# ScalarE, VectorE and GpSimd in source order in blocks 2 to 10, with attention and the slot softmax cut into steps over sixteen columns

## The chip, the cores and the metric

The kernel runs on one core of a Trainium2 chip. TensorE (PE) multiplies, ScalarE (ACT) evaluates functions and copies, VectorE (DVE) does element work, reductions and 32x32 transposes, GpSimd (POOL) does element work and issues some loads, and the queue of SyncE (SP) issues most transfers. The metric is the device time of the program in microseconds (us). A profiled execution also has a span, from its first instruction to its last.

## The reference: what is computed

```python
# attention within chunks of 64 positions, for each of 8 x 8 heads; S = 576, D = 64
scores = (1 / sqrt(64)) * q_c @ k_c.T
attn   = softmax(scores, axis=-1)
x      = (attn @ v_c)                      # -> 4608 tokens x 512
# a feed-forward layer, d_ff = 2048
h = x @ w_in
x = (h * sigmoid(1.702 * h)) @ w_out
# soft mixture of experts, 8 experts x 4 slots
logits = x @ phi                           # 4608 x 32
d = softmax over the tokens (axis 0);  c = softmax over the slots (axis 1)
slot_out = per expert: relu((d.T @ x) @ w1) @ w2
out = c @ slot_out
```

## The kernel before

The 4608 tokens go in twelve blocks of 384. Blocks 0 and 1 are written out by hand (FIRST), together with the conversion of the weights; blocks 2 to 10 run in `block`, whose order is the subject here; block 11 and the expert part (`tail`) follow.

A block has sixteen **columns**, one for each 128 of the 2048 hidden features. In each, `gemm(b, f)` runs twelve matmuls into one of three PSUM banks h (the input is split into two parts, xh and xl, and the weight likewise, so three products for each of four slices of the depth). ScalarE evaluates a tanh of h into gt, VectorE multiplies gt with h (which frees h) and transposes the result into g1. After every fourth column g1 is written to DRAM, and a block later `load_g` reads it back in another layout.

After the gemm of a column, `side(b, f)` adds what the table PLAN names for it. Each entry is a letter, an index and the column:

- **a, b, c**: three steps of attention for one group of 128 tokens of the next block. `attn_a` makes the scores s on TensorE, the maximum mx and the difference e on VectorE, the exponential on ScalarE, the sum sm and reciprocal rs on VectorE, and the product with rs on GpSimd. `attn_b` transposes e on TensorE into pt, and ScalarE copies it to pt_sb. `attn_c` multiplies with v on TensorE into x; ScalarE writes xh from it, VectorE writes xl. Indices 0 to 4 count groups from the first of the next block, so a3 and a4 are already of the block after that.
- **l**: a quarter of the logits (lp); l3 is the last quarter of the block before. ScalarE and VectorE split its result into lps.
- **s0, s1**: the slot softmax of the block before: lg on TensorE, then nm, d, cr, dt, lt, cm on VectorE and ScalarE; s1 ends it and writes ct to DRAM.
- **g, d**: `load_g` of the block before, and `dispatch`, the product dtg of dt with what was read back; VectorE adds it to acc.
- **w**: alternately the load and the conversion of one piece of w_out (wo), on ScalarE and VectorE.

Two PSUM places are shared. The scores s and the product x use one pair of banks ("sx"), so s waits until xh and xl of the x before it are written, and x waits until e of the s before it is written. The tag "m" is one bank for lg, pt and dtg.

What orders the work: in blocks 2 to 10 SyncE and TensorE run in source order (`manual_schedule`), while a scheduler that works ahead of time decides the order on ScalarE, VectorE and GpSimd. In FIRST, in block 11 and in the tail only SyncE keeps source order. Each engine takes its instructions one after the other in the order so fixed.

Of the kernel before, what the change touches and what calls it, by code (L numbers as in the profile page):

```python
# [8 lines left out]
F32 = mybir.dt.float32  # L9
# [3 lines left out]
ACTF = mybir.ActivationFunctionType  # L13
ALU = mybir.AluOpType
AX = mybir.AxisListType

T = 384
# [7 lines left out]
TABLE = {'9.15': 'wxx', '10.6': 'q', '10.11': 'vq', '10.15': 'v', '11.0': 'ssw', '11.8': 'sss', 'a': 'ss', 'b': 'ssss', 'e': 'pppppp'}  # L25
TABLE.update({f'11.{f}': TABLE.get(f'11.{f}', '') + 'w' for f in range(1, 16)})
EVAC = 'vvvvvvvvvvvvvvaa'
LAST = (('g0', 2), ('l3', 4), ('l0', 4), ('s0', 5), ('d0', 7), ('s1', 7), ('l1', 12), ('l2', 12))


PLAN = (('g0', 3), ('a2', 4), ('l3', 4), ('l0', 4), ('b1', 4), ('c0', 4), ('s0', 5), ('w0', 6), ('s1', 7), ('w1', 7), ('a3', 8), ('d0', 8), ('c1', 8), ('b2', 8), ('a4', 12), ('l1', 12), ('l2', 12), ('b3', 12), ('c2', 12), ('w2', 14), ('w3', 15))
NCV = 6
FIRST = "q0 A0 q1 z Li0 A1 q2 Li1 q3 v0 Li2 i0 A2 B0 C0 v1 B1 C1 phi v2 i1 Li3 B2 C2 v3 A3 q4 Li4 i2 Li5 Li6 g0 Li7 g1 i3 Li8 i4 i5 q5 Li9 v4 i6 Li10 g2 g3 Li11 A4 i7 B3 g4 Li12 i8 C3 Lo0r q6 i9 g5 Li13 g6 i10 B4 q7 A5r Li14 i11 g7 o0 g8 i12 i13 g9 Lo1r C4 v5 Lo2r A6r Li15 i14 B5 Lo3 Lo4r i15 o1 g10 C5 g11 g12 g13 o2 Lo5r v6 Lo6 g14 Lo7r Lo8r s o3 g15 G0 o4 Lo9 Lo10r o5 Lo11r o6 G1 Lo12r A7 o7 Lo13r o8 G2 G3 v7 o9 B6 c0 o10 v8 Lo14 G4 o11 o12 C6 d0 G5 o13 c1 t0 Lo15 t1 o14 m0 G6 G7 G8 t2 t3 B7 d1 c2 q8 q9 G9 o15 t4 l0 d2 c3 G10 l1 C7 m1 l2 A8r G11 t5 d3 l3 t6 G12 v9 B8 t7 G13 S t8 G14 D1 t9 t10 t11 C8 t12 G15 T t13 t14 q10 m2 t15 D3 v10 A9 q11 B9 A10 q12"
EPS = 1e-9
# [3 lines left out]
def attention_moe_softmoe_kernel(  # L38
# [12 lines left out]
    nc = tc.nc  # L51
# [7 lines left out]
    NCP = T // 128  # L59
# [11 lines left out]
    st_p = ctx.enter_context(tc.tile_pool(name="st", bufs=2))  # L71
    ps_h = ctx.enter_context(tc.tile_pool(name="ps_h", bufs=3, space=bass.MemoryType.PSUM))
    ps = ctx.enter_context(tc.tile_pool(name="ps", bufs=1, space=bass.MemoryType.PSUM))
# [4 lines left out]
    def pair_tile(name):  # L78
        return ps_x[0].tile([128, 2, 512], F32, tag="sx", name=name)
# [7 lines left out]
    def mid_tile(shape, name, dtype=F32):  # L87
        return mid.tile(shape, dtype, tag="m", name=name)
# [7 lines left out]
    sel_r = sel.rearrange("p j s -> p (j s)")  # L96
# [60 lines left out]
    qk_t, v_t, et, pt, xh, xl = {}, {}, {}, {}, {}, {}  # L157

    def load_qk(cp):
        if cp < NB * NCP:  # L160
            t = qkp.tile([128, 2, KD, 128], F32, tag="qk", name="qk")
            nc.sync.dma_start(out=t, in_=qk[cp].rearrange("p (a h c) -> p a h c", a=2, h=KD))
            qk_t[cp] = t

    def load_v(cp):
        if cp < NB * NCP:
            t = vpool.tile([128, KD, 128], F32, tag="v", name="v")
            nc.sync.dma_start(out=t, in_=vs[cp].rearrange("p (h c) -> p h c", h=KD))
            v_t[cp] = t

    def attn_a(cp, pool=False):
        t = qk_t.pop(cp)
        p = pair_tile("s")[:, :, 0:256].rearrange("p h (a k) -> p h a k", k=64)
        for hp in range(KD):
            for c in range(2):
                w = slice(64 * c, 64 * c + 64)
                for h in range(2):
                    r = slice(64 * h, 64 * h + 64)
                    nc.tensor.matmul(  # L179
                        out=p[w, h, hp, :], lhsT=t[r, 0, hp, w], rhs=t[r, 1, hp, w], start=True, stop=True  # L180
                    )
        mx = st_p.tile([128, 2, KD, 1], F32, tag="mx", name="mx")
        e = mid_tile([128, 2 * KD, 64], "e")
        nc.vector.tensor_reduce(out=mx, in_=p, axis=AX.X, op=ALU.max)  # L184
        nc.vector.tensor_tensor(  # L185
            out=e.rearrange("p (a h) k -> p h a k", h=2), in0=p, in1=mx.to_broadcast([128, 2, KD, 64]),
            op=ALU.subtract,
        )
        nc.scalar.activation(out=e, in_=e, func=ACTF.Exp, scale=0.125)  # L189
        sm = st_p.tile([128, 2 * KD, 1], F32, tag="sm", name="sm")  # L190
        nc.vector.tensor_reduce(out=sm, in_=e, axis=AX.X, op=ALU.add)
        nc.vector.tensor_scalar_add(out=sm, in0=sm, scalar1=EPS)
        rs = st_p.tile([128, 2 * KD, 1], F32, tag="rs", name="rs")
        nc.vector.reciprocal(out=rs, in_=sm)  # L194
        (nc.gpsimd if pool else nc.vector).tensor_tensor(  # L195
            out=e, in0=e, in1=rs.to_broadcast([128, 2 * KD, 64]), op=ALU.mult
        )
        et[cp] = e

    def attn_b(cp):  # L200
        e = et.pop(cp)
        if cp in (1, 2):
            p = ps_h.tile([128, KD, 128], F32, tag="h", name="pt1")
        else:
            p = ps.tile([128, KD, 128], F32, tag="m" if cp >= 3 * NCP + 1 else "pt", name="pt")
        for hp in range(KD):
            nc.tensor.transpose(p[:, hp, :], e[:, 2 * hp:2 * hp + 2, :].rearrange("p h k -> p (h k)"), ident)  # L207
        t = ptp.tile([128, KD, 128], F32, tag="p", name="pt_sb")
        nc.scalar.activation(out=t, in_=p, func=ACTF.Copy)
        pt[cp] = t  # L210
# [57 lines left out]
    def load_g(b):  # L268
        g2[b] = []
        for q in range(NG):  # L270
            t = slab_tile([128, 4, NCP, GF * 32], F32, f"g2_{q}")
            nc.sync.dma_start(
                out=t.rearrange("p q a c -> p (q a c)"), in_=g_dram.pop((b, q)).rearrange("b p q x -> (b p) (q x)")
            )
            g2[b].append([t[:, :, i, :] for i in range(NCP)])
# [28 lines left out]
    lp, lps = {}, {}  # L304

    def logits(b, g):
        if g == 0:
            lp[b] = ps.tile([128, T], F32, tag="lp" if b % 2 else "pt", name="lp") if b else ps_h.tile([128, T], F32, tag="h", name="lp0")
        for j in range(4):
            f = 4 * g + j  # L310
            nc.tensor.matmul(  # L311
                out=lp[b][32 * j:32 * (j + 1), :], lhsT=wp[:, f, :], rhs=gt[b, f],
                start=(g == 0), stop=(g == NG - 1),
            )
        if g == NG - 1:
            p = lp.pop(b)
            if b == NB - 1:
                lps[b] = [mid_tile([128, T], "lps")]
                nc.scalar.activation(out=lps[b][0], in_=p, func=ACTF.Copy)
                return  # L320
            lps[b] = [mid_tile([128, T], f"lps{i}", F32R) for i in range(2)]
            nc.scalar.activation(out=lps[b][0], in_=p, func=ACTF.Copy)
            nc.vector.tensor_tensor(out=lps[b][1], in0=p, in1=lps[b][0].bitcast(F32), op=ALU.subtract)

    stat, lg_t, d_t, dt_t = {}, {}, {}, {}

    def slots_a(b):
        lg = ps.tile([128, T], F32, tag="m", name="lg")
# [78 lines left out]
    def dispatch(b):  # L407
        dt, cr = dt_t.pop(b)
        g = g2.pop(b)
        p = ps.tile([128, 512], F32, tag="m", name="dtg")  # L410
        for i in range(NCP):
            for j in reversed(range(4)):
                nc.tensor.matmul(  # L413
                    out=p[32 * j:32 * (j + 1)], lhsT=dt[:, i, :], rhs=g[j][i], start=(i == 0), stop=(i == NCP - 1)
                )
        nc.vector.scalar_tensor_tensor(out=acc, in0=acc, scalar=cr, in1=p, op0=ALU.mult, op1=ALU.add)  # L416
# [80 lines left out]
    def more_wo():  # L497
        fn, i = wo_list.pop(0)
        fn(i)
# [138 lines left out]
    def side(b, f):  # L638
        for name, at in (LAST if b == NB - 1 else PLAN):
            if f != at:  # L640
                continue
            kind, i = name[0], int(name[1:])
            if kind == "l":
                if i == NG - 1:
                    logits(b - 1, i)
                else:
                    logits(b, i)
            elif kind == "s":
                (slots_a, slots_b)[i](b - 1)
            elif kind == "d":  # L650
                dispatch(b - 1)
            elif kind == "g":
                load_g(b - 1)
            elif kind == "w":
                if 1 < b < 10:
                    more_wo()
            elif (b + 1) * NCP + i < NB * NCP:
                cp = (b + 1) * NCP + i
                if kind == "a":
                    attn_a(cp, True)  # L660
                    load_qk(cp + 2)
                elif kind == "b":
                    attn_b(cp)
                else:
                    attn_c(cp)
                    load_v(cp + 2)
# [35 lines left out]
    def block(b):  # L702
        for f in range(NF):
            gemm(b, f)
            side(b, f)
            if b == NB - 1 and f:
                gemm_t(b, f - 1)
            at(f"{b}.{f}")


    SP, PE = mybir.EngineType.SP, mybir.EngineType.PE
# [3 lines left out]
        with tc.tile_pool(name="pro", bufs=1) as pro[0]:  # L715
            start()
    with tc.tile_pool(name="spare", bufs=NSPARE) as pro[1]:
        with tc.manual_schedule(engines={SP, PE}):
            more_wo()
            for b in range(2, NB - 1):  # L720
                block(b)
        pair.__exit__(None, None, None)
        with tc.manual_schedule(engines={SP}):
            with tc.tile_pool(name="ps_t", bufs=1, space=bass.MemoryType.PSUM) as ps_x[0]:
                block(NB - 1)
                tail()
# [60 lines left out]
```

## Time and profile before

| what | value |
|---|---|
| time, median of 3 runs | 745.45 us (743.87 to 746.79) |
| the profiled execution's own time | 743.41 us |
| its span | 741.6 us |
| TensorE busy, share of the span | 656.0 us, 88% |
| VectorE busy | 445.5 us, 60% |
| ScalarE busy | 240.5 us, 32% |
| GpSimd busy | 107.5 us, 14% |
| mean granted TensorE clock | 0.965 |

Busy times overlap, since the engines work side by side. The end of the program is set by whichever engine the others wait for; a wait on that engine is time, a wait elsewhere is not. The granted clock is the share of TensorE's full rate that it was given.

### The profile page before, as it was taken

What the parts mean: (1) busy time and instruction counts of PE and PEld (TensorE: products, weight loads), DVE (VectorE), ACT (ScalarE), POOL (GpSimd) and SP (SyncE); (2) the same over time, 40 slices, a digit from 0 to 9 for tenths busy, and PEclk for the clock granted to TensorE, in tenths of its full rate; (3) what the DMA queues carried; (4) which work ended last, traced back from release to release, by engine and by line L of the source; (5) the groups of instructions that cost most, each with busy time, mean ns of one, the idle gap of its engine ahead of it and who ended that gap; (6) DMA issues with size and microseconds to landing.
All of it is one profiled execution on the core that took longest, in us unless ns stands there. A gap on an engine that the chain in (4) does not pass through costs nothing.

```text
span 741.6 us, 15661 instructions
## 1 busy us (share of the span) xinstructions
PE 656.0 (88%) x6462; PEld 536.4 (72%) x6462; DVE 445.5 (60%) x963; ACT 240.5 (32%) x517; POOL 107.5 (14%) x153
## 2 busy tenths in 40 slices
PE   3888999888998998989989989989899799988982
PEld 2777975666796896876968968968769689854641
DVE  6698762667557666676585576666765644531122
ACT  4466352523323332332333233323322222221132
POOL 1235000000100000000001000000000111435650
PEclk9998999999999999999999999999999999999997
DMA  7845264257657476575586574765855858979998
GB/s 246 324 179 207 86 241 157 58 145 267 189 131 261 140 215 230 132 277 146 132 279 178 126 257 147 225 219 130 280 142 163 281 155 294 342 269 324 385 393 367
DMA packets 64919, 161.66 MB, mean 218 GB/s; under 512 B 12880, under 2 KB 34512, under 8 KB 64848
## 3 DMA queue, kind: packets, MB, share of 16 engines
q1 hardware_dynamic: 54496, 123.43, 52.3%
q0 software_dynamic: 10352, 37.23, 13.8%
q8 instruction: 51, 0.84, 0.5%
q14 instruction: 20, 0.16, 0.1%
HBM read 119.14 MB, written 41.48 MB: 217 GB/s over the span
## 4 chain that ended last, share of the span: by engine, by line
PE 76%; DVE 8%; issue 6%; DMA 5%; ACT 2%; SPq 1%; POOL 0%; DVEq 0%; ACTq 0%; POOLq 0%
PE h L241 17%; PE h L242 16%; PE h L243 16%; PE dtg L413 6%; PE lp L311 5%; DMA g<-g_dram 3%; PE s L179 3%; PE pt L207 2%; PE x L225 2%; PE h1p L571 2%; DVE cv L107 1%; PE gtp L293 1%; DMA out_dram<-o 1%; DVE acc L416 1%; PE fp L591 1%
## 5 line engine op out<-in xcount | busy, mean ns | idle before, releaser
L241 PE MATMUL h<-xh,w 128*128 128x384 f32 x768 | 265.5, 346 | 2.7 <-DVE gt L246 2.0
L242 PE MATMUL h<-xl,w 128*128 128x384 f32 x768 | 260.4, 339 | 0.0
L243 PE MATMUL h<-xh,w 128*128 128x384 f32 x768 | 259.8, 338 | 0.0
L246 DVE SCALAR_TENSOR_TENSOR gt<-gt,h 128x384 f32<-128x384 f32 x192 | 105.6, 550 | 132.8 <-ACT gt L245 132.5
L245 ACT ACTIVATE gt<-h 128x384 f32<-128x384 f32 x192 | 94.0, 491 | 256.1 <-PE h L243 255.1
L241 PEld LDWEIGHTS h<-xh,w 128*128 128x128 f32 x768 | 146.1, 190 | 10.6 <-issue 4.4
L242 PEld LDWEIGHTS h<-xl,w 128*128 128x128 f32 x768 | 146.2, 190 | 1.2 <-issue 0.8
L243 PEld LDWEIGHTS h<-xh,w 128*128 128x128 f32 x768 | 146.0, 190 | 0.0
L195 POOL TENSOR_TENSOR e<-e,rs 128x512 f32<-128x512 f32 x28 | 30.1, 1075 | 454.2 <-DVE rs L194 454.2
L253 DVE STREAM_TRANSPOSE g<-gt 128x384 f32<-128x384 f32 x160 | 89.0, 569 | 3.6
L179 PE MATMUL s<-qk 64*64 64x64 f32 x1152 | 28.1, 242 | 34.3 <-issue 24.0
L179 PEld LDWEIGHTS s<-qk 64*64 64x64 f32 x1152 | 23.0, 150 | 44.5 <-issue 37.3
L413 PE MATMUL dtg<-g,dt 128*32 128x512 f32 x264 | 44.7, 831 | 5.2 <-DMA g<-g_dram 3.8
L189 ACT ACTIVATE e<-e 128x512 f32<-128x512 f32 x36 | 22.7, 631 | 66.1 <-DVE e L185 66.1
L225 PEld LDWEIGHTS x<-pt_sb,v 64*64 64x64 f32 x1152 | 21.9, 142 | 29.8 <-issue 20.0
L311 PE MATMUL lp<-gt,wp 128*32 128x384 f32 x384 | 40.7, 493 | 0.4 <-ACT wp L154 0.4
L225 PE MATMUL x<-pt_sb,v 64*64 64x64 f32 x1152 | 26.5, 232 | 13.1 <-PE pt L207 5.0
L475 POOL DMA_DIRECT2D w<-in_moe_w_dram x44 | 23.7, 543 | 91.2 <-PE x L225 26.0
L231 ACT ACTIVATE xh<-x 128x512 fp32r<-128x512 f32 x36 | 21.4, 595 | 39.0 <-PE x L225 39.0
L184 DVE TENSOR_REDUCE mx<-s 128x8 f32<-128x512 f32 x36 | 24.1, 670 | 16.3 <-PE s L179 16.3
L232 DVE TENSOR_TENSOR xl<-x,xh 128x512 fp32r<-128x512 f32 x36 | 24.4, 677 | 12.0 <-ACT xh L231 11.8
L413 PEld LDWEIGHTS dtg<-g,dt 128*32 128x32 f32 x264 | 10.1, 142 | 29.2 <-issue 27.0
(104 smaller groups left out, 603.0 us busy)
## 6 DMA issues: line engine op xcount, KB each, us to landing
g_dram<-g SPq DMA_DIRECT2D x160, 192.0 KB, 3.1
g<-g_dram SPq DMA_DIRECT2D x40, 768.0 KB, 8.4
qk<-in_qk_dram SPq DMA_DIRECT2D x36, 512.0 KB, 5.6
w<-in_moe_w_dram POOLq DMA_DIRECT2D x70, 256.0 KB, 5.2
w<-in_moe_w_dram POOLq DMA_DIRECT2D x27, 512.0 KB, 7.2
v<-in_v_dram SPq DMA_DIRECT2D x36, 256.0 KB, 5.8
stg<-in_moe_w_in_dram SPq DMA_DIRECT2D x16, 512.0 KB, 6.7
stg<-in_moe_w_out_t_dram SPq DMA_DIRECT2D x16, 512.0 KB, 5.6
```

The costliest lines, as they stand in the source:

```text
L179: nc.tensor.matmul(out=p[w, h, hp, :], lhsT=t[r, 0, hp, w], rhs=t[r, 1, hp, w], start=True, stop=True)
L195: (nc.gpsimd if pool else nc.vector).tensor_tensor(out=e, in0=e, in1=rs.to_broadcast([128, 2 * KD, 64]), op=ALU.mult)
L225: nc.tensor.matmul(out=x[64 * z:64 * z + 64, h, a, w], lhsT=t[r, 2 * a + z, w], rhs=p[r, 2 * a + z, w], start=True, stop=True,)
L232: nc.vector.tensor_tensor(out=yl, in0=x, in1=yh.bitcast(F32), op=ALU.subtract)
L241: nc.tensor.matmul(out=h, lhsT=a, rhs=xh[b][:, k, :], start=(k == 0), stop=False)
L242: nc.tensor.matmul(out=h, lhsT=a, rhs=xl[b][:, k, :], start=False, stop=False)
L243: nc.tensor.matmul(out=h, lhsT=l, rhs=xh[b][:, k, :], start=False, stop=(k == KD - 1))
L245: nc.scalar.activation(out=t, in_=h, func=ACTF.Tanh, scale=0.851)
L246: nc.vector.scalar_tensor_tensor(out=t, in0=t, scalar=1.0, in1=h, op0=ALU.add, op1=ALU.mult)
L253: nc.vector.transpose(out=g1[q][:, :, :, 32 * j:32 * (j + 1)], in_=t.rearrange("p (a b c) -> p b a c", b=4, c=32))
L311: nc.tensor.matmul(out=lp[b][32 * j:32 * (j + 1), :], lhsT=wp[:, f, :], rhs=gt[b, f], start=(g == 0), stop=(g == NG - 1),)
L413: nc.tensor.matmul(out=p[32 * j:32 * (j + 1)], lhsT=dt[:, i, :], rhs=g[j][i], start=(i == 0), stop=(i == NCP - 1))
```

## The change

All of ScalarE, VectorE and GpSimd now keep source order in blocks 2 to 10 as well. So that a step's later part does not stand in front of the next columns, the steps are cut: `attn_a` becomes `attn_s` (scores, maximum, difference; letter a) and `attn_e` (exponential to the product with rs; letter e), and the first half of the slot softmax becomes four functions `slots_0` to `slots_3` (letter S; S4 is the old `slots_b`). PLAN is written anew: its 21 entries stood in nine of the columns, 14 of them in columns 4, 8 and 12; its 27 entries now stand in thirteen. In LAST, the table of block 11, the dispatch moves from column 7 to column 9.

```diff
-LAST = (('g0', 2), ('l3', 4), ('l0', 4), ('s0', 5), ('d0', 7), ('s1', 7), ('l1', 12), ('l2', 12))
-PLAN = (('g0', 3), ('a2', 4), ('l3', 4), ('l0', 4), ('b1', 4), ('c0', 4), ('s0', 5), ('w0', 6), ('s1', 7), ('w1', 7), ('a3', 8), ('d0', 8), ('c1', 8), ('b2', 8), ('a4', 12), ('l1', 12), ('l2', 12), ('b3', 12), ('c2', 12), ('w2', 14), ('w3', 15))
+LAST = (('g0', 2), ('l3', 4), ('l0', 4), ('s0', 5), ('s1', 7), ('d0', 9), ('l1', 12), ('l2', 12))
+PLAN = (('b1', 1), ('w2', 1), ('w3', 1), ('g0', 2), ('a2', 2), ('l3', 3), ('l0', 3), ('e2', 3), ('c0', 4), ('S0', 5), ('a3', 6), ('S1', 6), ('b2', 7), ('e3', 7), ('S2', 7), ('c1', 8), ('S3', 8), ('S4', 9), ('a4', 10), ('d0', 10), ('b3', 11), ('e4', 11), ('c2', 12), ('l1', 12), ('l2', 12), ('w0', 13), ('w1', 13))
...
     def attn_a(cp, pool=False):
+        attn_s(cp)
+        attn_e(cp, pool)
+
+    def attn_s(cp):
...
+        et[cp] = e
+
+    def attn_e(cp, pool):
+        e = et[cp]
...
+    def slots_0(b):
+        lg = ps.tile([128, T], F32, tag="m", name="lg")
+        for i, v in enumerate(lps.pop(b)):
+            nc.tensor.matmul(out=lg, lhsT=sel_r, rhs=v, start=(i == 0), stop=(i == 1))
+        nm = st_p.tile([128, 1], F32, tag="nm", name="nm")
+        nc.vector.tensor_reduce(out=nm, in_=lg, axis=AX.X, op=ALU.max, negate=True)
+        nc.vector.tensor_tensor(out=nm, in0=nm, in1=stat[b - 1][0], op=ALU.min)
+        lt = st_p.tile([128, NCP, 32], F32, tag="lt", name="lt")
+        for j in range(4):
+            r = slice(32 * j, 32 * j + 32)
+            nc.vector.transpose(out=lt[r], in_=lg[r, :].rearrange("p (a j c) -> p a j c", j=4, c=32)[:, :, j, :])
+        sm_t[b] = lg, nm
+        lg_t[b] = lt
+
+    def slots_1(b):
+        lg, nm = sm_t.pop(b)
+        s = st_p.tile([128, 1], F32, tag="sum", name="sum")
+        d = mid_tile([128, T], "d")
+        nc.scalar.activation(out=d, in_=lg, func=ACTF.Exp, bias=nm, accum_out=s)
+        cr = st_p.tile([128, 1], F32, tag="cr", name="cr")
+        nc.scalar.activation(out=cr, in_=stat[b - 1][0], func=ACTF.Exp, scale=-1.0, bias=nm)
+        sm_t[b] = d, nm, s, cr
+
+    def slots_2(b):
+        d, nm, s, cr = sm_t.pop(b)
+        dt = st_p.tile([128, NCP, 32], F32, tag="dt", name="dt")
+        for j in range(4):
+            r = slice(32 * j, 32 * j + 32)
+            nc.vector.transpose(out=dt[r], in_=d[r, :].rearrange("p (a j c) -> p a j c", j=4, c=32)[:, :, j, :])
+        nc.vector.scalar_tensor_tensor(out=s, in0=stat[b - 1][1], scalar=cr, in1=s, op0=ALU.mult, op1=ALU.add)
+        dt_t[b] = dt, cr
+        stat[b] = nm, s
+        lt = lg_t[b]
+        cm = st_p.tile([128, NCP, 1], F32, tag="cm", name="cm")
+        nc.vector.tensor_reduce(out=cm, in_=lt, axis=AX.X, op=ALU.max)
+        nc.vector.tensor_tensor(out=lt, in0=lt, in1=cm.to_broadcast([128, NCP, 32]), op=ALU.subtract)
+
+    def slots_3(b):
+        nc.scalar.activation(out=lg_t[b], in_=lg_t[b], func=ACTF.Exp)
...
+            elif kind == "S":
+                (slots_0, slots_1, slots_2, slots_3, slots_b)[i](b - 1)
...
                 if kind == "a":
-                    attn_a(cp, True)
+                    attn_s(cp)
                     load_qk(cp + 2)
+                elif kind == "e":
+                    attn_e(cp, True)
...
-        with tc.manual_schedule(engines={SP, PE}):
+        with tc.manual_schedule(engines={SP, PE, mybir.EngineType.Activation, mybir.EngineType.DVE, mybir.EngineType.Pool}):
```

What the instructions' order becomes is shown at three places. Line numbers are those of each kernel's own file, so tanh is L245 before and L253 now.

**ScalarE, from the columns before column 4 to column 8 of a middle block.** `gt<-h` is the tanh of one column (x8: eight columns), `xh<-x` belongs to c0 of column 4. Before:

```order
L245 ACTIVATE gt<-h 128x384 x8
L322 ACTIVATE lps_3594<-lp 128x384
L189 ACTIVATE e<-e 128x512
L209 ACTIVATE pt_sb<-pt 128x512
L245 ACTIVATE gt<-h 128x384
L103 ACTIVATE wo<-wo_3458 128x512
L351 ACTIVATE d,sum<-lg,nm 128x384
L355 ACTIVATE cr<-nm 128x1
L245 ACTIVATE gt<-h 128x384 x2
L377 ACTIVATE lt<-lt 128x96
L245 ACTIVATE gt<-h 128x384
L231 ACTIVATE xh<-x 128x2x2x128
```

and now:

```order
L253 ACTIVATE gt<-h 128x384 x2
L330 ACTIVATE lps_3582<-lp 128x384
L198 ACTIVATE e<-e 128x512
L253 ACTIVATE gt<-h 128x384
L239 ACTIVATE xh<-x 128x2x2x128
L253 ACTIVATE gt<-h 128x384 x2
L354 ACTIVATE d,sum<-lg,nm 128x384
L356 ACTIVATE cr<-nm 128x1
L253 ACTIVATE gt<-h 128x384
L217 ACTIVATE pt_sb<-pt 128x512
L198 ACTIVATE e<-e 128x512
L253 ACTIVATE gt<-h 128x384
```

The copy of c0 to xh stood behind the tanh of column 8, four tanhs after that of column 4; it now stands right behind the tanh of column 4, and the slot softmax's `d` one tanh later than the column of its lg.

**VectorE, columns 5 to 8 of a middle block.** `gt<-gt,h` is the multiplication that frees a bank h, `g<-gt` the transposition, `xl<-x,xh` the second half of an attention step c. Before (from the slot softmax on):

```order
L246 SCALAR_TENSOR_TENSOR gt<-gt,h 128x384
L376 TENSOR_TENSOR lt<-lt,cm 128x96
L246 SCALAR_TENSOR_TENSOR gt<-gt,h 128x384
L383 TENSOR_REDUCE cs<-lt 128x3
L384 TENSOR_SCALAR cs<-cs 128x3
L385 RECIPROCAL cs<-cs 128x3
L386 TENSOR_TENSOR lt<-lt,cs 128x96
L388 STREAM_TRANSPOSE ct_b<-lt 128x96
L246 SCALAR_TENSOR_TENSOR gt<-gt,h 128x384
L253 STREAM_TRANSPOSE g_3558<-gt 128x12x32 x2
L232 TENSOR_TENSOR xl<-x,xh 128x2x2x128
L253 STREAM_TRANSPOSE g_3558<-gt 128x12x32 x2
L253 STREAM_TRANSPOSE g_3748<-gt 128x12x32
```

and now (column 7 to the step c of column 8):

```order
L254 SCALAR_TENSOR_TENSOR gt<-gt,h 128x384
L261 STREAM_TRANSPOSE g_3614<-gt 128x12x32
L200 TENSOR_REDUCE sm<-e 128x8
L201 TENSOR_SCALAR sm<-sm 128x8
L203 RECIPROCAL rs<-sm 128x8
L364 STREAM_TRANSPOSE dt<-d 32x96 x4
L365 SCALAR_TENSOR_TENSOR sum<-sum,cr 128x1
L370 TENSOR_REDUCE cm<-lt 128x3
L371 TENSOR_TENSOR lt<-lt,cm 128x96
L254 SCALAR_TENSOR_TENSOR gt<-gt,h 128x384
L261 STREAM_TRANSPOSE g_3773<-gt 128x12x32
L240 TENSOR_TENSOR xl<-x,xh 128x2x2x128
```

Before, the xl of column 4 came behind the slot softmax and two transpositions of later columns. Now column 7 holds the multiplication, the transposition, the sum of an attention step (sm, rs) and the dt half of the slot softmax, and the xl shown last is that of c1 in column 8.

**VectorE, the start of block 2.** The rows begin with the maximum of A10, the last attention step of FIRST, and end with the product of e with rs that b1 needs. Before:

```order
L184 TENSOR_REDUCE mx<-s 128x8
L185 TENSOR_TENSOR e<-s,mx 128x2x4x64
L246 SCALAR_TENSOR_TENSOR gt<-gt,h 128x384 x2
L253 STREAM_TRANSPOSE g_1788<-gt 128x12x32
L191 TENSOR_REDUCE sm<-e 128x8
L253 STREAM_TRANSPOSE g_1788<-gt 128x12x32
L192 TENSOR_SCALAR sm<-sm 128x8
L246 SCALAR_TENSOR_TENSOR gt<-gt,h 128x384
L194 RECIPROCAL rs<-sm 128x8
L253 STREAM_TRANSPOSE g_1788<-gt 128x12x32
L195 TENSOR_TENSOR e<-e,rs 128x512
```

and now:

```order
L189 TENSOR_REDUCE mx<-s 128x8
L190 TENSOR_TENSOR e<-s,mx 128x2x4x64
L254 SCALAR_TENSOR_TENSOR gt<-gt,h 128x384
L261 STREAM_TRANSPOSE g_1788<-gt 128x12x32
L200 TENSOR_REDUCE sm<-e 128x8
L254 SCALAR_TENSOR_TENSOR gt<-gt,h 128x384
L201 TENSOR_SCALAR sm<-sm 128x8
L261 STREAM_TRANSPOSE g_1788<-gt 128x12x32
L203 RECIPROCAL rs<-sm 128x8
L204 TENSOR_TENSOR e<-e,rs 128x512
L105 TENSOR_SCALAR wo<-wo 128x512
L108 SCALAR_TENSOR_TENSOR wo<-wo_1770,wo 128x512
```

Between A10's difference and its product there stood three multiplications and three transpositions of block 2; now there are two of each. The conversion of wo (the last two rows) stood ahead of the step before, A9, and now stands behind A10. TensorE's order changes with it: b1, which needs A10's product, stood behind five gemms of block 2 (column 4) and now stands behind two (column 1), directly after A10's scores; and A9's transposition, which had ten matmuls of the third gemm of block 2 ahead of it, now stands behind the second gemm.

## Rows read from the trace of the kernel before

**Rows 1.** Waits of TensorE over the whole span: us in total, times, longest.

```profile
PE s L179 <- issue: 24.0, 8, 3.0
PE x L225 <- PE pt L207: 5.0, 8, 0.6
PE dtg L413 <- DMA g<-g_dram: 3.8, 1, 3.8
```

**Rows 2.** Chain of work, middle block: start us, us, what.

```profile
331.56 3.01 issue
334.56 0.69 PE s L179 x32
335.26 4.45 PE dtg L413 x24
339.73 0.76 DVE acc L416
350.21 1.43 PE lp L311 x16
352.24 0.61 issue
353.54 0.37 PE h L241
353.91 0.18 PE h L242
```

**Rows 3.** The same chain, ten microseconds earlier.

```profile
322.00 0.67 PE x L225 x32
```

**Rows 4.** Timeline of ScalarE in that block.

```profile
331.58 0.49 ACT L245 ACTIVATE gt<-h 128x384 f32<-128x384 f32 x1 [0.40 <-PE h L243]
331.96 0.59 ACT L231 ACTIVATE xh<-x 128x512 fp32r<-128x512 f32 x1
```

**Rows 5.** Timeline of VectorE in that block.

```profile
333.81 0.65 DVE L232 TENSOR_TENSOR xl<-x,xh 128x512 fp32r<-128x512 f32 x1
343.96 0.56 DVE L246 SCALAR_TENSOR_TENSOR gt<-gt,h 128x384 f32<-128x384 f32 x1 [2.29 <-ACT gt L245]
344.55 0.58 DVE L253 STREAM_TRANSPOSE g<-gt 128x384 f32<-128x384 f32 x1
352.05 0.69 DVE L185 TENSOR_TENSOR e<-s,mx 128x512 f32<-128x512 f32 x1
353.72 0.68 DVE L191 TENSOR_REDUCE sm<-e 128x8 f32<-128x512 f32 x1
378.43 1.11 DVE L362 STREAM_TRANSPOSE dt<-d 32x96 f32<-32x96 f32 x4
```

**Rows 6.** Stretches: us, busy PE, PEld, DVE, ACT, POOL; clock; DMA share; GB/s.

```profile
333.00:334.00 1.00, 0.00 (x0) 0.00 (x0) 1.00 (x3) 0.00 (x0) 0.00 (x0) 1.00 0.43 164
336.00:337.00 1.00, 1.00 (x12) 0.32 (x8) 0.97 (x2) 0.00 (x0) 0.00 (x0) 0.50 0.72 164
162.00:164.00 2.00, 1.63 (x9) 1.63 (x10) 2.00 (x5) 0.52 (x1) 0.00 (x0) 1.00 0.49 197
```

**Rows 7.** Chain of work in block 11: the last dispatch.

```profile
664.02 2.90 PE dtg L413 x24
```

**Rows 8.** Timeline of TensorE at the start of block 2.

```profile
158.73 0.66 PE L207 MATMUL pt<-ident,e 128*128 128x128 f32 x4 [0.33 <-DVE e L195]
159.67 0.69 PE L179 MATMUL s<-qk 64*64 64x64 f32 x32
162.37 0.44 PE L241 MATMUL h<-xh,w 128*128 128x384 f32 x1 [2.00 <-DVE gt L246]
```

**Rows 9.** Timeline of VectorE there: A10's product.

```profile
165.37 0.65 DVE L195 TENSOR_TENSOR e<-e,rs 128x512 f32<-128x512 f32 x1
```

**Rows 10.** Line L424, the load of wo: from issue to landing.

```profile
DMA to landing us min/median/max: 4.0/4.7/5.8
```

**Rows 11.** Line L272, the strips read back by load_g: from issue to landing.

```profile
DMA to landing us min/median/max: 5.3/8.4/13.0
```

More of the change, by code (lines that the diff above doesn't have):

```diff
@@ L197, in attn_a @@
         )
-        et[cp] = e
     def attn_b(cp):
@@ L323, in logits @@
             nc.vector.tensor_tensor(out=lps[b][1], in0=p, in1=lps[b][0].bitcast(F32), op=ALU.subtract)
-    stat, lg_t, d_t, dt_t = {}, {}, {}, {}
+    stat, lg_t, d_t, dt_t, sm_t = {}, {}, {}, {}, {}
+    def slots_0(b):
[34 more added lines that the diff above has]
+        nc.scalar.activation(out=lg_t[b], in_=lg_t[b], func=ACTF.Exp)
     def slots_a(b):
```

## The prediction

> **What bounds the kernel now.** I read first who TensorE waits for over the whole span, then the chain of work of one middle block, then the timelines of the engines that the chain names, and last the granted clock in short stretches.
>
> The waits of TensorE [rows 1] are few kinds: the scores s of the attention waited 24.0 us in eight waits of some 3 us, the product x 5.0 us in eight, and one dispatch 3.8 us for a transfer. In blocks 2 to 9 one wait of each of the first two kinds stands in each block. In the chain [rows 2] the first is the "issue" of 3.01 us, just before the scores of a3 in column 8. The chain names no releaser, the other views do: the scores need the banks in which x of c0 lies. That x was computed at 322.00 [rows 3], but ScalarE copied it to xh only at 331.96 [rows 4], behind the tanh of column 8 at 331.58, and VectorE's xl ended at 333.81 + 0.65 = 334.46 [rows 5], 0.10 us before the scores start. So TensorE waits for the place of two instructions in two queues, not for their work. The wait of 0.61 us before an x [rows 2] ends 0.10 us after VectorE's e of the scores just before it, at 352.05 + 0.69 = 352.74 [rows 5]: the same pair of banks, the other way round.
>
> The long wait costs more than itself. [...] An idle time of 2.00 us at the start of block 2 [rows 8] left the clock at 1.00 [rows 6].
>
> **What comes back.** The copies to xh and xl now stand directly behind their own x, no longer behind four later tanhs.
>
> - a3 stands two columns behind c0. Two gemms of twelve matmuls at 0.17 to 0.18 us [rows 2] are 4.2 us; xh and xl need about 1.4 (0.59 and 0.65 with the hand-overs). The eight waits go: 24.0 us.
> - Without that idle time I take the dispatch at full clock: 4.45 - 2.90 = 1.55 us, in nine blocks 14.0 us. In block 10 the idle time is the wait for the transfer, so it must go as well.
> - That transfer (the strips of load_g) is issued one column earlier and needed two columns later. Eight gemms, 16.8 us, lie between, and the slowest strip took 13.0 us [rows 11]: 3.8 us come back.
> - No x stands directly behind the scores any more; at least one gemm lies between: 5.0 us.
> - The dispatch is no longer followed by a transposition that needs its bank back; the 0.76 us of VectorE's acc [rows 2] leave the chain, and an x of 0.67 us [rows 3] that ran beside it enters: 0.1 us, in nine blocks 0.9.
>
> Together 47.7 us.
>
> **What it costs.**
>
> - *More changes of shape.* The first gemm matmul after an x takes 0.37 us, the next 0.18 [rows 2]. Before, two groups of side work in a block ended with x. Now two x (columns 4 and 8) and two groups of logits (3 and 12) are followed by a gemm, and two scores (2 and 6), whose 64x64 matmuls are nearest to x. Four more at 0.2 us, in nine blocks: 7.2 us. The bounds are two more (only logits and x cost it: 3.6) and seven more (transpositions, lg and dispatch too: 12.6).
> - *The start of block 2.* A10's scores ended at 159.67 + 0.69 = 160.36 [rows 8] and its product at 165.37 + 0.65 = 166.02 [rows 9], 5.66 us later. One multiplication and one transposition less lie in between (0.56 + 0.58 [rows 5]), so 4.5 us; and b1, which needs the product, now stands directly behind the scores. TensorE idles 4.5 us there instead of 2.00. A9's transposition waited 0.33 us [rows 8]; the ten matmuls that stood ahead of it (1.7 us) are gone, and A9's product comes earlier by the conversion of wo (about 1.1 us, an estimate from two element rows such as 0.56 and 0.65): it waits 0.6 longer. That is 3.1 us. The idle time is longer than 3.01, so I add one fall of the clock, 1.55, and the sum is 4.7. At best, if the product came sooner, it is 0.
> - *The quarter l0 in column 3* now stands directly behind the gemm whose gt it needs. Tanh and multiplication take 0.49 + 0.56 [rows 4, 5], with hand-overs 1.15; TensorE meanwhile does l3 and three quarters of l0, seven eighths of 1.43 [rows 2], so 1.25. Nothing, but the cover is only 0.1 us.
> - *VectorE in column 7.* Multiplication, transposition, sm and dt are 0.56 + 0.58 + 0.68 + 1.11 [rows 5], and six short ones I put at 0.9 (an estimate): 3.8 us against 2.7 of TensorE. The xl of c1 comes 0.56 + 0.58 + 0.65 later and is needed by a4. Counted from the end of gemm 7, VectorE starts at 0.6 and is done at 6.2; TensorE comes to a4 after a transposition, three gemms and an x, 0.66 + 6.3 + 0.67 = 7.6. The cover is 1.4 us, from which some 0.4 of backlog of column 5 goes.
> - GpSimd's products have at least three columns until the transposition that needs them: nothing.
>
> [...] The new table makes more and smaller groups. [...]
>
> **The sum.** 47.7 - 7.2 - 4.7 = 35.8 us. The profiled execution took 743.41 us, its span 741.6 and 1.8 around it; it becomes 707.6. It lies 2.0 below the median of the runs, 745.45, which becomes **709.7 us**.
>
> **The rivals.**
>
> - *VectorE is late after column 7.* Some thirty instructions of it stand between column 5 and the xl of c1; if each took 0.08 us longer than I lay them, 2.4 us, the cover of about 1.0 is used up and a4 waits 1.4 us in eight blocks: 11 us, 721 us. For it: the column's sum is above TensorE's. Against it: columns 8 to 10 leave room. [...]
> [...]
> - *It does little*: the scores wait for something other than xl, and the waits stay where they are: some 745 us. Against it stand the two hand-overs of 0.10 us.
> - *Slower: the load of wo holds up ScalarE in column 1.* That load is issued behind the conversion of column 13, about 2.8 us after gemm 13 ends, and ScalarE comes to the conversion in column 1 after four gemms, a transposition and a copy, at 9.6: the load has 6.8 us. It took 4.0 to 5.8 [rows 10]. In source order a late load holds back the tanh behind it, then gt, then l0, almost one for one. If it took as long as the slowest strip, 13.0 [rows 11], that is 6.2 us in the seven blocks 3 to 9, 43 us: 753 us. It turns the sign from 12.1 us on, where 7 x 5.3 exceeds 35.8.
> - *Better*: only logits and x cost the 0.2 (3.6 back) and the start of block 2 hides half: 703 us and below.
>
> **Chances.** Forecast (703 to 716) 0.60; VectorE late 0.17; clock 0.07; better 0.08; little 0.04; slower 0.04. The range 700 to 723 holds the forecast, most of VectorE's case and the better one, some 8 in 10. A change within 0.5% (3.7 us) is about what a measurement of this kernel cannot tell from none. Faster 0.92, same 0.04, slower 0.04.
>
> **What the changed profile would show.** The 3 us waits before the scores are gone; xh starts within a microsecond of its x; the dispatch takes 2.9 us and the clock stays at 1.00 through the middle blocks; a middle block is some 4.5 us shorter (40.5 in nine). One wait of 4 to 5 us stands at the start of block 2, before b1. No dispatch waits for a strip. The forecast would be wrong if TensorE waited in each block for VectorE before a4 or before l0, or for a gt behind a late conversion of wo, or if the first matmul after each small group cost clearly more than 0.2 us.

## The result, and the profile after the change

The changed kernel takes 705.33 us (median of 4 runs, 704.88 to 708.01); the kernel before, run beside it, 745.19 us (median of 4, 743.87 to 746.79). The ratio is 0.9472, interval 0.9441 to 0.9502: 39.9 us less. The profiled execution went from 743.41 to 708.01 us (35.4 less), its span from 741.6 to 706.2. The forecast was 709.7 by the median and 707.6 for the profiled execution.

The page of the changed kernel: TensorE is now busy for 92% of the span (88% before), with nearly the same busy time, and the row of its granted clock has a 9 in all slices but two, the one in which block 2 starts (8) and the last (7). The mean granted clock is 0.982 (0.965 before).

```profile
PE 652.3 (92%) x6462; PEld 534.7 (76%) x6462; DVE 446.6 (63%) x963; ACT 238.7 (34%) x517; POOL 107.3 (15%) x153
...
PEclk9999999998999999999999999999999999999997
```

TensorE's waits over the whole span (us in total, times, longest). None of the three lines of [rows 1] is left. The longest line now, 8.4 us for two loads of qk, was there before with 7.8. The new one holds the 5.1 us at the start of block 2:

```profile
PE pt L215 <- DVE e L204: 6.0, 2, 5.1
```

One stretch of 47 us in the middle blocks: TensorE is busy all of it, at a clock of 1.00 (columns as in [rows 6]). A wait between the matmuls of one group, as that of l0 further down, does not show as idle time here.

```profile
294.00:341.00 47.00, 47.00 (x458) 40.25 (x459) 33.92 (x75) 15.64 (x32) 3.13 (x3) 1.00 0.67 211
```

The chain of a middle block, from the scores of column 2 to those of the next block (start us, us, what; most of the twelve gemm matmuls of a column are left out). It is TensorE from end to end.

```profile
307.07 0.62 PE s L184 x32
307.69 0.38 PE h L249
...
309.98 2.00 PE lp L319 x16
311.98 0.37 PE h L249
...
314.26 0.62 PE x L233 x32
314.89 0.38 PE h L249
...
317.18 0.35 PE lg L339 x2
317.52 0.17 PE h L249
...
319.61 0.62 PE s L184 x32
320.23 0.38 PE h L249
...
322.52 0.44 PE pt L215 x4
322.95 0.18 PE h L249
...
325.06 0.63 PE x L233 x32
325.69 0.38 PE h L249
...
330.06 0.62 PE s L184 x32
330.68 2.71 PE dtg L462 x24
333.40 0.37 PE h L249
...
338.85 1.43 PE lp L319 x16
340.28 0.37 PE h L249
...
353.43 0.62 PE s L184 x32
```

Three things are to be seen. The scores of a3 and a4 (319.61, 330.06) follow their gemm without a wait, where [rows 2] have 3.01 us. The dispatch takes 2.71 us against 4.45. And 353.43 - 307.07 = 46.36 us is one block; before, the 3.01 us "issue" stood at 331.56 [rows 2] and again at 382.58, 51.02 us later. More rows of the chain before, with that block's transpositions:

```profile
340.63 0.63 PE pt L207 x4
...
351.63 0.60 PE pt L207 x4
...
372.43 0.59 PE pt L207 x4
...
382.58 3.01 issue
```

ScalarE's timeline beside it: xh follows its x at 314.26 by 0.08 us after x ends (314.88); [rows 3, 4] had almost ten microseconds between the two.

```profile
314.96 0.60 ACT L239 ACTIVATE xh<-x 128x512 fp32r<-128x512 f32 x1 [0.16 <-PE x L233]
```

### The profile page after: what moved, and what is told of

It is laid out like the page before. It is cut to its first block, busy times and chain, and to the rows that moved or that the text cites. A ratio compares the mean times of both kernels' runs of the same rounds, so it can differ in the third digit from the quotient of the medians.

```text
span 706.2 us, 15678 instructions
## 1 busy us (share of the span) xinstructions
PE 652.3 (92%) x6462; PEld 534.7 (76%) x6462; DVE 446.6 (63%) x963; ACT 238.7 (34%) x517; POOL 107.3 (15%) x153
## 4 chain that ended last, share of the span: by engine, by line
PE 79%; DVE 7%; DMA 7%; issue 2%; ACT 2%; POOL 1%; DVEq 0%; POOLq 0%; ACTq 0%
PE h L249 20%; PE h L250 18%; PE h L251 18%; PE lp L319 6%; PE dtg L462 4%; DMA w<-in_moe_w_dram 4%; PE s L184 3%; PE x L233 3%; PE pt L215 2%; PE gtp L301 1%; DMA qk<-in_qk_dram 1%; DVE cv L108 1%; DMA out_dram<-o 1%; POOL w L530 1%; PE dtg L449 1%
## 5 line engine op out<-in xcount | busy, mean ns | idle before, releaser
L249 PE MATMUL h<-xh,w 128*128 128x384 f32 x768 | 271.7, 354 | 0.7 <-ACT xh L239 0.7
L251 PE MATMUL h<-xh,w 128*128 128x384 f32 x768 | 260.4, 339 | 0.0
L253 ACT ACTIVATE gt<-h 128x384 f32<-128x384 f32 x192 | 94.1, 491 | 311.1 <-PE h L251 311.0
L261 DVE STREAM_TRANSPOSE g<-gt 128x384 f32<-128x384 f32 x160 | 92.5, 578 | 5.2
L319 PE MATMUL lp<-gt,wp 128*32 128x384 f32 x384 | 45.9, 493 | 0.4 <-ACT wp L155 0.4
L524 POOL DMA_DIRECT2D w<-in_moe_w_dram x44 | 23.6, 541 | 61.5 <-PE h L251 28.4
L462 PE MATMUL dtg<-g,dt 128*32 128x512 f32 x264 | 30.6, 596 | 1.4 <-DVE dt L407 1.4
L215 PE MATMUL pt<-ident,e 128*128 128x128 f32 x144 | 23.9, 292 | 8.5 <-DVE e L204 6.0
L530 POOL DMA_DIRECT2D w<-in_moe_w_dram x53 | 28.3, 537 | 17.9 <-DMA w<-in_moe_w_dram 11.8
```

The lines of the kernel that those rows point to most:

```text
L249: nc.tensor.matmul(out=h, lhsT=a, rhs=xh[b][:, k, :], start=(k == 0), stop=False)
L251: nc.tensor.matmul(out=h, lhsT=l, rhs=xh[b][:, k, :], start=False, stop=(k == KD - 1))
L253: nc.scalar.activation(out=t, in_=h, func=ACTF.Tanh, scale=0.851)
L261: nc.vector.transpose(out=g1[q][:, :, :, 32 * j:32 * (j + 1)], in_=t.rearrange("p (a b c) -> p b a c", b=4, c=32))
L319: nc.tensor.matmul(out=lp[b][32 * j:32 * (j + 1), :], lhsT=wp[:, f, :], rhs=gt[b, f], start=(g == 0), stop=(g == NG - 1),)
L462: nc.tensor.matmul(out=p[32 * j:32 * (j + 1)], lhsT=dt[:, i, :], rhs=g[j][i], start=(i == 0), stop=(i == NCP - 1))
```

## The experiments

In the first four the question is which part of the change does it and whether VectorE's cover is as thin as the forecast says; in the others, what its two visible costs are.

**The old table in source order.** The kernel before, with only the list of engines changed.

```diff
-        with tc.manual_schedule(engines={SP, PE}):
+        with tc.manual_schedule(engines={SP, PE, mybir.EngineType.Activation, mybir.EngineType.DVE, mybir.EngineType.Pool}):
```

> The table and the whole steps of the kernel before, with ScalarE, VectorE and GpSimd in source order in blocks 2 to 10. Theory (order and table are both needed): the copies xh and xl of c0 stand behind their x, so the 3 us wait before a3 goes; but the whole attention step and the whole slot softmax now stand in front of the next columns on VectorE, and in columns 4, 8 and 12 a product x stands right behind the scores of the same column, so x waits for VectorE's e there, several us in column 8. I expect 730 to 755 us, no clear gain. Rival (the order alone is the gain, the table is ornament): about 710 us.

771.00 us (769.51 to 772.18), ratio 1.0362 (1.0333 to 1.0391): slower than expected. A block takes 54.5 us. TensorE's waits, then ScalarE's timeline around column 7, and VectorE's and TensorE's in column 8:

```profile
PE x L225 <- issue: 26.8, 9, 3.8
PE pt L207 <- DVE acc L416: 13.7, 9, 1.9
```

```profile
344.15 0.28 ACT L377 ACTIVATE lt<-lt 128x96 f32<-128x96 f32 x1 [2.88 <-DVE lt L376]
344.34 0.47 ACT L245 ACTIVATE gt<-h 128x384 f32<-128x384 f32 x1
```

```profile
350.94 0.69 DVE L185 TENSOR_TENSOR e<-s,mx 128x512 f32<-128x512 f32 x1
```

```profile
351.73 0.93 PE L225 MATMUL x<-pt_sb,v 64*64 64x64 f32 x32 [3.17 <-issue]
```

The wait before a3's scores is gone, as the theory had it, and TensorE waits before the x of column 8 instead, until 0.10 us after VectorE's e ends (350.94 + 0.69 = 351.63). That e is late because, uncut, the slot softmax stands in one piece in three queues: the tanh behind it (344.34) waits for lt, lt for VectorE, and VectorE's work of the following columns is pushed back with it. After the wait the gemm matmuls take 0.32 us each instead of 0.17, until 358.9 us; the mean granted clock from 322 to 377 us is 0.94. Source order alone costs 27 us.

**The new table under the scheduler.** The changed kernel with `engines={SP, PE}`.

> The changed kernel, but the scheduler again decides the order on ScalarE, VectorE and GpSimd. In the order that it makes, xh of c0 stands behind the tanh of column 6 and a conversion. Theory (the place of xh in ScalarE's queue is what TensorE waits for): a3 of column 6 waits 2 to 4 us once a block for it, and where it does the clock falls again: 725 to 750 us. Rival (the new table alone removes the wait, since it spreads the steps): 703 to 710 us.

770.60 us (767.83 to 772.92), ratio 1.0358 (1.0315 to 1.0401), also above what was expected. TensorE's waits, ScalarE's and VectorE's timelines in a middle block, and TensorE's own there:

```profile
PE s L184 <- issue: 34.4, 7, 5.1
```

```profile
336.29 0.58 ACT L239 ACTIVATE xh<-x 128x512 fp32r<-128x512 f32 x1
```

```profile
339.18 0.65 DVE L240 TENSOR_TENSOR xl<-x,xh 128x512 fp32r<-128x512 f32 x1
```

```profile
329.42 0.69 PE L233 MATMUL x<-pt_sb,v 64*64 64x64 f32 x32
...
339.93 1.13 PE L184 MATMUL s<-qk 64*64 64x64 f32 x32 [5.11 <-issue]
```

x ended at 330.11, xh began 6.2 us later, xl ended at 339.83, and the scores began 0.10 us after that: the hand-over of 0.10 us of [rows 2, 5] again, in another order. The scheduler still puts the two copies late; the new table leaves only two columns for them, not four, so the wait grows from 3.0 to 5.1 us. The clock falls again, as expected: its mean from 322 to 377 us is 0.94, these scores take 1.13 us instead of 0.62, and the gemm matmuls behind them 0.32 instead of 0.17 until 344.9 us.

**ScalarE alone in source order.** The changed kernel with `engines={SP, PE, mybir.EngineType.Activation}`.

> The changed kernel with ScalarE in source order and VectorE and GpSimd left to the scheduler. In VectorE's order xl of c0 stands behind the maximum and four transpositions of the slot softmax, still ahead of the scores of column 6. Theory (ScalarE's place for xh was the cause, VectorE followed it): 703 to 712 us, no 3 us wait before the scores. Rival (VectorE's order is the cause as much): above 720 us.

720.51 us (716.42 to 722.88), ratio 0.9678 (0.9638 to 0.9719). The same line of TensorE's waits is left with 1.5 us at most:

```profile
PE s L184 <- issue: 10.6, 7, 1.5
```

```profile
325.86 0.69 DVE L240 TENSOR_TENSOR xl<-x,xh 128x512 fp32r<-128x512 f32 x1
```

```profile
326.65 0.69 PE L184 MATMUL s<-qk 64*64 64x64 f32 x32 [1.51 <-issue]
```

It is now xl alone that comes late: it ends at 326.55, 0.10 us before the scores begin. A block takes 48.3 us. With the new table ScalarE's order is worth 50.1 us (770.60 to 720.51), that of VectorE and GpSimd the last 15.2. The theory's 703 to 712 us was too low, and the rival's "above 720 us" is just met: ScalarE's queue is not the whole of it.

**The dt transposes three times.** Two extra sets of transposes in column 7 load VectorE alone; the output is the same.

```diff
-            nc.vector.transpose(out=dt[r], in_=d[r, :].rearrange("p (a j c) -> p a j c", j=4, c=32)[:, :, j, :])
+            for _ in range(3):
+                nc.vector.transpose(out=dt[r], in_=d[r, :].rearrange("p (a j c) -> p a j c", j=4, c=32)[:, :, j, :])
```

> The changed kernel with the four transpositions to dt done three times over in column 7 of each block (same result), 2.2 us more of VectorE there. Theory (a cover of 1.0 to 1.4 us before a4 needs xl): a4 waits 0.8 to 1.2 us in most blocks, 712 to 717 us. Rival one (VectorE is already on the edge): all of it is paid, 2.2 us in nine blocks, 725 us. Rival two (the cover is larger than laid out): 705 us.

716.23 us (715.34 to 718.76), ratio 0.9632 (0.9603 to 0.9662): as expected. TensorE's waits, and VectorE's timeline:

```profile
PE s L184 <- DVE xl L240: 9.4, 9, 1.1
```

```profile
328.70 3.50 DVE L365 STREAM_TRANSPOSE dt<-d 32x96 f32<-32x96 f32 x12
```

The twelve transposes take 3.50 us instead of 1.07 for four, 2.43 more; a4's scores wait 1.1 us. So 1.3 us were hidden (2.43 - 1.1). That is VectorE's cover in the changed kernel.

**b1 in column 3 of block 2.** Only in block 2, b1 moves from column 1 to column 3.

```diff
+FIRST_PLAN = tuple(x for x in PLAN if x[0] in ('w2', 'w3')) + (('g0', 2), ('a2', 2), ('b1', 3)) + tuple(x for x in PLAN if x[0] not in ('w2', 'w3', 'g0', 'a2', 'b1'))
...
-        for name, at in (LAST if b == NB - 1 else PLAN):
+        for name, at in (LAST if b == NB - 1 else FIRST_PLAN if b == 2 else PLAN):
```

> The changed kernel, but in block 2 alone b1 stands in column 3 instead of column 1, behind two more gemms. Theory (the start of block 2 costs a wait of 5.1 us for A10's product and then a stretch of some 6.5 us at half clock, 3 us more): both go, 696 to 699 us, and no granted clock below 1.00 at the start of block 2. Rival one (only the wait comes back, the low clock has another cause): 700 us. Rival two (the wait moves to the scores or to l0 of that block): 703 to 706 us.

704.96 us (700.46 to 706.10, six runs), ratio 0.9479 (0.9440 to 0.9519): a miss by the median, which lies in the range of rival two. In the trace the wait of 5.1 us is gone, the clock at the start of block 2 is 1.00, and from VectorE's first acc to that of block 2 it is 37.9 us instead of 42.6. That is 4.7 less, not the 8 of the theory, since other waits have come in its place, as rival two said: 1.6 us before the scores of a2, which now stand directly behind A10's, 1.3 us for A10's product, and 0.8 us in l0. So 4.7 us were saved in the trace and the median did not show them; the last group takes that up.

**l3 and l0 in column 4**, one column later, in all middle blocks.

```diff
-PLAN = (... ('l3', 3), ('l0', 3), ('e2', 3), ('c0', 4), ...)
+PLAN = (... ('e2', 3), ('l3', 4), ('l0', 4), ('c0', 4), ...)
```

> The changed kernel with l3 and l0 in column 4, ahead of c0, instead of column 3. Theory (l0 waits 0.57 us in each block for the gt of the gemm just before it, and a group less costs one first matmul of 0.38 instead of 0.17): 0.77 us in nine blocks, 6.9 us: 698 to 699 us; the 16 matmuls take 1.43 us again. Rival one (the 2.00 us of that group are no wait, but the shape of a group that starts with l3): only 1.8 us come back, 703.5 us. Rival two (lps comes later and lg in column 5 waits for it): 705 us or more.

697.96 us (696.79 to 704.42), ratio 0.9394 (0.9357 to 0.9431): as expected. The chain:

```profile
313.05 1.43 PE lp L319 x16
314.48 0.62 PE x L233 x32
315.10 0.37 PE h L249
```

lp takes 1.43 us instead of 2.00, and since x now follows it directly, one 0.2 us of a first gemm matmul goes too: a block takes 45.6 us, 0.8 less.

**Both moves together.**

> Both edits of the two runs before: b1 of block 2 in column 3, l3 and l0 in column 4. Theory: the two add up, some 8 and 7 us: 689 to 693 us. Rival: they share a wait at the start of block 2, so that less than 12 us come back together.

695.91 us (694.84 to 696.99), ratio 0.9349 (0.9310 to 0.9387), 2.9 us above what was expected and the fastest version measured. By the median 9.4 us come back together, less than 12 as the rival said. By the traces the two moves add up: from VectorE's first acc to its last it is 478.6 us in the changed kernel, 473.9 with b1 moved, 471.7 with l3 and l0 moved and 465.8 with both, so 4.6, 6.9 and 12.8 us less. A shared wait is not seen, but each trace is one execution.

**The changed kernel again, and b1 in columns 3 and 4, on one chip.**

> The changed kernel once more, unaltered, on the same chip as the two runs below, since the order b1 in column 3 of block 2 had shortened the stretch of block 2 by 4.7 us in its trace and the median by only 0.4 us, in runs made at another time. Theory: the stretch before block 2 differs by some 2.5 us from execution to execution, and the two medians of different chips or hours hide the gain; here the median is 704 to 707 us, and b1 in column 3 is 3 to 5 us below it. Rival: the time saved in block 2 is given back in the executions that are not profiled; then the two medians agree within 1 us here too.

> b1 in column 3 of block 2, as before. Theory: 3 to 5 us below the changed kernel of the same chip, some 701 us. Rival (given back): within 1 us of it.

> b1 one column later still, in column 4 of block 2, directly ahead of c0. If A10's product is the only thing that held up TensorE there, column 3 already hid all of its 5.1 us and column 4 gives the same time within 1 us. Rival: in column 4 the transposition stands directly ahead of x, which needs ScalarE's copy pt_sb of it, and TensorE waits about 1 us for that: 1 us slower than column 3.

The changed kernel took 705.55 us (704.97 to 711.74), b1 in column 3 701.56 (698.92 to 706.28), in column 4 705.22 (702.60 to 706.83), six runs each; the ratios to before are 0.9497 (0.9457 to 0.9537), 0.9442 (0.9401 to 0.9482) and 0.9474 (0.9439 to 0.9510). Column 3 is 4.0 below the changed kernel, as the theory of the run variation had it; the intervals overlap. The median of column 4 fits neither figure written for it. In its trace the stretch of block 2 is 38.3 us, only 0.4 longer than with column 3: A10's product is not waited for any more, but l0 waits 1.9 us for VectorE's gt. The rest lies earlier: A10's scores, which come before the first difference in the order of instructions, begin at 160.44 instead of 154.63. Both kernels run the same order until there. Stretches of the first part, column 3 and then column 4:

```profile
45.00:50.00 5.00, 5.00 (x59) 4.73 (x58) 5.00 (x9) 2.56 (x6) 0.95 (x2) 1.00 0.01 2
...
65.00:70.00 5.00, 5.00 (x29) 5.00 (x30) 5.00 (x11) 4.54 (x10) 2.77 (x2) 1.00 0.40 156
```

```profile
45.00:50.00 5.00, 5.00 (x22) 4.97 (x21) 4.82 (x9) 1.38 (x3) 1.40 (x2) 0.66 0.00 0
...
65.00:70.00 5.00, 5.00 (x47) 4.50 (x48) 4.93 (x10) 2.81 (x6) 1.43 (x2) 0.61 0.81 325
```

Instructions in the same order ran at a lower granted clock in these two stretches (0.66 and 0.61 against 1.00). The clock of column 3 falls just before them too, to a mean of 0.66 from 40 to 45 us (0.66 for column 4 as well) and of 0.82 from 60 to 65 us (0.70), but it is back sooner. In 30 to 145 us the mean clock is 0.97 for column 3 and 0.93 for column 4. The kernel with b1 in column 3 is the same in both of its groups, and its medians are 704.96 and 701.56. In the first group the executions with a mean clock of 0.986 and 0.987 took 701.92 and 700.46 us, those with 0.978 took 705.38 to 706.10. So medians differ by 3.4 us without any change of the kernel, and the 4.0 us of column 3 are not shown by the medians alone; the stretch of block 2, 4.1 to 4.7 us shorter in two traces of each kernel, shows them.

## Why the prediction was right

**What bound the kernel** was named rightly: TensorE waited for the places of xh and xl in two queues. The wait goes when, and only when, the copies come forward: with the new table and the scheduler they stay late and the wait grows to 5.1 us; with ScalarE in order xl is still late and 1.5 us are left; with all three none. With the old table in source order it goes as well, but another wait takes its place. The rival "it does little" is out.

**The sum for a block**, the forecast's terms against the two chains:

| term | forecast | measured |
|---|---|---|
| a3's wait | 3.0 | 3.01 |
| dispatch at full clock | 1.55 | 4.45 - 2.71 = 1.74 |
| wait before x | 0.6 | 0.61 |
| acc in the chain (339.73 to 340.63), less the x that enters | 0.1 | 0.90 - 0.63 = 0.27 |
| transpositions pt, three | 0 | 3 x 0.17 = 0.5 |
| first gemm matmuls | -0.8 | -5 x 0.2 = -1.0 |
| l0 waits for gt | 0 | -(2.00 - 1.43) = -0.57 |
| sum | 4.5 | 4.56 |

The block became 51.02 - 46.36 = 4.66 us shorter. The sum is right because errors of both signs met. The steps that were mis-sized:

- *l0 "nothing, but the cover is only 0.1 us"*: the wait is 0.57, some 5 us in nine blocks. The place was right, the cover was not: VectorE's gt ends at 311.10, 1.1 us after lp begins, as forecast, and the last weights of l0 are loaded at 311.15 (the row below; PEld is the weight load of TensorE). TensorE could have had them sooner than the 1.25 us laid down: with the quarters of column 12, which wait for nothing, it is at the last weights 0.67 us after the first (PEld at 338.78 and 339.45). The run that moved l3 and l0 gave 0.57 back at that place, so this is shown.
- *"Four more at 0.2 us"*: it is seven matmuls of 0.37 or 0.38 a block against two before, five more. Scores, lp and x cost it as laid down, the dispatch too; lg and pt don't (317.52 and 322.95 in the chain above).
- *The dispatch*: 2.71, not the 2.90 of [rows 7]. The 4.45 of [rows 2], which falls into the clock of 0.50 of [rows 6], was longer by 1.74, not by 1.55.
- *The transpositions*: directly behind a gemm one takes 0.44 us; the three of the block before stood behind other groups and took 0.63, 0.60 and 0.59. The forecast left that out. It is much the same price as that of a first gemm matmul (0.15 to 0.19 and 0.2 us). If the two are one, the block before paid it five times and the block now seven times: two more, not four.

```profile
311.15 0.14 PEld L319 LDWEIGHTS lp<-gt,wp 128*32 128x32 f32 x2 [0.44 <-DVE gt L254]
```

The wait for the strips of load_g is gone from the waits, as forecast.

**The start of block 2** was put at 4.7 us and cost some 6.3. TensorE's timeline there, then stretches of 2 us:

```profile
156.50 0.66 PE L215 MATMUL pt<-ident,e 128*128 128x128 f32 x4 [0.95 <-DVE e L204]
...
162.84 1.12 PE L215 MATMUL pt<-ident,e 128*128 128x128 f32 x4 [5.06 <-DVE e L204]
```

```profile
160.00:162.00 2.00, 0.00 (x0) 0.00 (x0) 2.00 (x6) 0.00 (x0) 0.00 (x0) 0.83 0.41 168
...
166.00:168.00 2.00, 2.00 (x14) 1.56 (x17) 0.40 (x1) 0.10 (x1) 0.00 (x0) 0.50 0.42 45
168.00:170.00 2.00, 2.00 (x40) 1.93 (x37) 1.54 (x3) 0.39 (x1) 0.00 (x0) 0.96 0.85 307
```

The wait for A10's product is 5.06 us (forecast 4.5, idle before 2.00 [rows 8]), and A9's transposition waits 0.95 instead of 0.33. The wait was put 0.6 us too low, but the term most mis-sized is "one fall of the clock, 1.55": TensorE works at 0.50 from 162.84 to about 168.2, and what it does in that time is longer by 0.68 (the transposition, 1.12 against 0.44), 1.76 (twelve gemm matmuls at 0.32 against 0.17) and 0.17 (scores, 0.79 against 0.62), by the chains: 2.6 us. 3.1 + 0.6 + 2.6 = 6.3. From the first acc to the last the profiled executions differ by 35.5 us; nine blocks at 4.66 would be 41.9, which leaves 6.4. With b1 in column 3 the clock has 1.00 there and 4.1 to 4.7 us come back, the rest going into the smaller waits named above.

**The median** came out 4.4 us below the forecast, though the profiled execution was met within 0.4 us (707.6 and 708.01). The step that failed is the offset of 2.0 us from profile to median, carried over as if it belonged to the kernel. In the kernel after, the profiled execution lies 2.7 above the median, and in its second group of runs 0.5 (706.01 and 705.55); VectorE's first acc came at 148.4 to 154.8 us in the versions with the new table, before anything in them differs.

**The rivals.** *VectorE late after column 7* was a real mechanism, 1.3 us away where the forecast had put about 1.0: the run with tripled dt shows its wait at its place, a4, at 1.1 us. *Clock* (0.07) was the chance that the clock falls once a block, as it did before. That did not happen: the smaller groups left no idling in the middle blocks beyond the 0.57 us in a group, and the middle stretch has 1.00. *The load of wo* held up nothing: between 190 and 620 us TensorE's waits hold one line, of 0.8 us, for another step.

```profile
PE gtp L301 <- DVE g L305: 0.8, 1, 0.8
```

## What to carry to other kernels

When a busy engine waits, look where the instruction that releases it stands in its queue, not only how long it takes; here the place of two copies of 0.6 us held TensorE up by 4.75 us a block (3.01, and 1.74 by the clock). Source order and a table that spreads short steps belong together: each alone cost 26 to 27 us, both gave 39.9. Price a step that needs the product of the step just ahead of it by the whole hand-over (5.06 us of waiting for A10's product here), and compare versions that differ by a few microseconds by the stretches of their traces as well as by medians.

## What was not expected of the hardware

- After 3.01 us of idle time the dispatch lost 1.74 us to the clock of 0.50, so it ran at it for about 3.5 us; after 5.06 us of idle time TensorE stayed at 0.50 for some 5.3 us. The runs don't show what sets that length. After the 1.5 us of idle time with ScalarE alone in order the scores took 0.69 us, and after the 1.1 us with dt tripled they took 0.69 and the dispatch behind them 2.78, by the timelines, just as in the changed kernel at a clock of 1.00 (0.69 and 2.78).
- The same instructions, in the same order, reached block 2 at times 5.8 us apart, with granted clocks of 1.00 and of 0.61 and 0.66 in the same stretches. What starts it was not tried, and stays open; so does why the version with both moves gained only 2.05 us by the median over the one with l3 and l0 moved, where the stretch of block 2 in their profiles is 36.1 against 42.0 us.
- A transposition of the same four matmuls takes 0.44 us behind a gemm and 0.59 to 0.63 behind lp or the dispatch, and the gemm matmul behind it 0.17 or 0.18, not 0.37.
